# A piece of q moved from the plain load queue to the casting queue, and the beginning of an attention and SwiGLU kernel put in a new order

## Chip, cores, metric

One core of one Trainium2 chip. The metric is the device time of one execution in microseconds (us). Executions are compared by the mean of their fast runs; a run counts as slow when it is over 1.5% above the fastest of the same kernel. For every run the mean granted clock of TensorE is on record too (the share of its full clock that the engine was given, 1.00 being all of it), and it turns out to matter here. Times inside an execution are microseconds from the start of its span.

## The reference

```python
def _attn_ref(q, k, v):                    # each 8 x 8 x 576 x 64, float32
    def phi(x, c, s):                      # c, s: cosine and sine of pi/2 * position / 576
        r = np.maximum(x, 0.0)
        return np.concatenate([r * c, r * s], axis=-1)
    q_p, k_p = phi(q, cos_w, sin_w), phi(k, cos_w, sin_w)
    kv = np.einsum('bhsf,bhsd->bhfd', k_p, v)
    z = np.sum(k_p, axis=2)
    num = np.einsum('bhsf,bhfd->bhsd', q_p, kv)
    den = np.einsum('bhsf,bhf->bhs', q_p, z)[..., None] + 1e-06
    return num / den
# its output, as 4608 x 512, is the x of:
def _moe_ref(x, w_gate, w_val, w_out):     # 512 x 1536, 512 x 1536, 1536 x 512
    g = x @ w_gate
    return (g / (1 + np.exp(-g)) * (x @ w_val)) @ w_out
```

## The kernel before

The feed-forward products dominate, and TensorE is busy with them from about 18 us to the end. What concerns us is the beginning: until the first tiles of attention output (x) exist, TensorE has nothing to multiply. Loads come by two ways: SyncE's plain queue brings float32 (`first`), GpSimd's queue casts to bf16 on the way (`raw`). q of the first batch is cut into slots 0 to 8; two slots make one tile of 128 rows.

```python
    CUT = (4, 7)
    first = {"q": consts.tile([P, G, CUT[0], D], FP32, name="first_q")}
    # ... homes of the first v and k, float32, in buffers that are used later ...
    def load_first(nm, gs, lo=0, hi=NC):              # plain, no cast
        nc.sync.dma_start(out=first[nm][:, gs, lo:hi]..., in_=source(0, nm)[:, gs, lo * D:hi * D])
    load_first("v", slice(0, 2))
    load_first("v", slice(2, 4))
    load_first("q", slice(0, G), 0, 2)                # tile 0
    load_first("k", slice(0, 2))
    load_first("k", slice(2, 4), 0, KCUT)
    load_first("k", slice(2, 4), KCUT, NC)
    load_first("q", slice(0, G), 2, 4)                # tile 1, behind k
    # ...
    nc.gpsimd.tensor_copy(out=hold, in_=first["v"][:, 1, 0, 0:1])   # casting queue starts when v is there
    load_slots(0, "q", CUT[0], NW)                    # tiles 2 and 3, cast to bf16
    load_w(0, 1)                                      # then the weights
    # ...
    def turn_q(t):                                    # transposes of tile t
        ...
                if t < 2:                             # from the cast copy qf: 4 products of 128 columns
                    nc.tensor.transpose(out=ps[:, y]..., in_=qf[:, c, j]..., identity=ident)
                    continue
                for i in range(2):                    # from raw: 8 products with 64 columns as weights
                    nc.tensor.transpose(out=ps[i * D:(i + 1) * D, y], in_=raws[0, "q"][:, 2 * j + i, 2 * t + c], ...)
```

The order in which the engines get the work of the beginning is a list of words. `cq` casts a q slot, `tq` transposes a tile, `qr` relus it, `qw` weights it with cosine and sine, `rk` relus k, `kv` makes the k·v products, `kvo` copies them out, `a` makes a tile's attention products, `den`, `rec`, `x` divide, `xt` and `xc` transpose x and copy it, `G` and `V` are gate and value products, `s` and `m` silu and multiplication, and `z` are fillers: products with zeros that only keep TensorE busy.

```python
    words = """
        cq0@act cq1@act tq0 qr0@dve rk1.0@act rk0.0@dve qw0.0 qw0.1 z6 kv0.0 rk2.0@act rk3.0@dve rk2.1@act
        kv1.0 kvo01@dve rk3.1@act cq3@dve kv1.1 cq2@dve kvo00@dve tq1 kvo10@act a0.0 qr1@dve kvo11@act qw1.1
        z2 a0.1 qw1.0 tq2 den0 rec0 a1.0 x0.0 qr2@act tq3 x0.1 xt0.0 a1.1 qw2.0 xc0.0@act xt0.1 qw2.1
        xc0.1@act den1 z2 a2.0 rec1 qr3@act G1.0 ...
    """.split()
```

Gate and value products of narrow tiles share one accumulator bank:

```python
    def ffn_mm(tg, fc, lo=0, hi=GH, which=(0, 1)):
        # ...
                both = take(1, ("f", tg, fc, lo))
                st["f", tg, fc, lo] = [both[:, 0:n], both[:, n:2 * n]]    # gate half, value half
```

## Time and profile before

| | before |
|---|---|
| time, first three runs (median) | 327.97 us |
| span of the profiled run, its mean clock | 326.1 us, 1.00 |
| TensorE busy | 98% |
| k·v products end | 12.69 us |
| last piece of q (slots 2 and 3) lands, tile 1 starts | 13.67, 14.40 us |
| last product of the beginning ends | 30.17 us |
| first output product | 43.16 us |
| first long product group (512 columns) | 57.13 us |

The rows from the end of the k·v products on are the markers by which the runs below are compared. The page of a profile has mean shares; the beginning is read from the chain of work in order of time (who released whom), from the timeline (start, length, engine, line, and in brackets the idle time ahead and what ended it) and from the time that transfers took to land. In these views PE is TensorE and PEld its weight loads, DVE is VectorE, ACT ScalarE, POOL GpSimd, SP SyncE, a q behind the name the engine's instruction queue, and L316 line 316 of the kernel. The lines stand in the prediction.

### The profile page before, as it was taken

What the parts mean: (1) busy time and instruction counts of PE and PEld (TensorE: products, weight loads), DVE (VectorE), ACT (ScalarE), POOL (GpSimd) and SP (SyncE); (2) the same over time, 40 slices, a digit from 0 to 9 for tenths busy, and PEclk for the clock granted to TensorE, in tenths of its full rate; (3) what the DMA queues carried; (4) which work ended last, traced back from release to release, by engine and by line L of the source; (5) the groups of instructions that cost most, each with busy time, mean ns of one, the idle gap of its engine ahead of it and who ended that gap; (6) DMA issues with size and microseconds to landing.
All of it is one profiled execution on the core that took longest, in us unless ns stands there. A gap on an engine that the chain in (4) does not pass through costs nothing.

```text
span 326.1 us, 6192 instructions
## 1 busy us (share of the span) xinstructions
PE 318.7 (98%) x2459; PEld 165.0 (51%) x2470; DVE 182.3 (56%) x367; ACT 132.8 (41%) x248; POOL 34.1 (10%) x57
## 2 busy tenths in 40 slices
PE   8799999999999999999999999999999999999995
PEld 4488855454545444544454445444454445444443
DVE  7594857885575655575557555655664145423420
ACT  7353456843463336423543344343432133213311
POOL 6654300002001100020002000200000000000000
PEclk9999999999999999999999999999999999999999
DMA  7999999398867997799598949795921411140014
GB/s 259 224 199 197 207 204 211 62 132 137 162 117 95 163 140 146 110 157 158 121 124 127 181 110 136 108 184 116 138 51 34 99 32 32 36 105 21 2 32 97
DMA packets 71660, 40.51 MB, mean 124 GB/s; under 512 B 46672, under 2 KB 66384, under 8 KB 71632
## 3 DMA queue, kind: packets, MB, share of 16 engines
q1 hardware_dynamic: 49808, 22.55, 39.0%
q0 software_dynamic: 21664, 17.44, 35.2%
q8 instruction: 19, 0.31, 0.4%
q10 hardware_dynamic: 160, 0.13, 0.1%
q14 instruction: 9, 0.07, 0.1%
HBM read 37.75 MB, written 9.44 MB: 145 GB/s over the span
## 4 chain that ended last, share of the span: by engine, by line
PE 94%; DMA 3%; SPq 1%; issue 0%; ACT 0%; DVE 0%; ACTq 0%; DVEq 0%
PE banks L503 57%; PE banks L539 28%; DMA first_q<-in_q_dram 3%; PE banks L276 3%; PE banks L390 2%; SPq L116 1%; PE banks L475 1%; PE banks L434 1%; PE banks L372 1%; PE banks L558 1%; PE banks L264 0%; PE banks L149 0%; ACT ob L561 0%; PE banks L351 0%; DVE qf L339 0%
## 5 line engine op out<-in xcount | busy, mean ns | idle before, releaser
L514 DVE TENSOR_TENSOR ht<-sg,banks 128x512 bf16<-128x512 bf16 (+2 forms) x122 | 76.0, 625 | 67.2 <-PE banks L503 60.9
L509 ACT ACTIVATE sg<-banks 128x512 bf16<-128x512 f32 (+2 forms) x122 | 66.9, 548 | 113.8 <-PE banks L503 108.7
L503 PE MATMUL banks<-xT,wv_sb 128*128 128x512 bf16 (+2 forms) x488 | 112.8, 355 | 0.0
L503 PE MATMUL banks<-xT,wg_sb 128*128 128x512 bf16 (+2 forms) x488 | 112.8, 355 | 0.0
L539 PE MATMUL banks<-wo_sb,ht 128*128 128x512 bf16 x409 | 93.5, 379 | 0.6
L503 PEld LDWEIGHTS <-wv_sb 128*128 128x128 bf16 x488 | 47.1, 98 | 46.4
L503 PEld LDWEIGHTS <-wg_sb 128*128 128x128 bf16 x488 | 45.7, 98 | 41.5
L539 PEld LDWEIGHTS <-ht 128*128 128x128 bf16 x420 | 40.0, 98 | 45.2 <-issue 0.4
L546 ACT COPY ob<-banks 128x512 f32<-128x512 f32 x18 | 10.6, 586 | 51.4 <-PE banks L539 49.4
L232 DVE TENSOR_TENSOR r_q<-raw_q,tab 128x1152 bf16<-128x1152 bf16 x24 | 17.9, 753 | 20.2 <-ACT raw_q L215 20.2
L546 DVE COPY ob<-banks 128x512 f32<-128x512 f32 x17 | 11.7, 691 | 28.9 <-PE banks L539 28.0
L236 DVE TENSOR_TENSOR v<-raw_v,tab 128x1152 bf16<-128x1152 bf16 x31 | 23.0, 751 | 0.3 <-ACT raw_v L570 0.3
L411 DVE TENSOR_TENSOR x<-banks,rec 128x512 bf16<-128x512 f32 (+1 forms) x32 | 21.5, 674 | 1.1
L714 POOL COPY hold<-phit 1x2 bf16<-1x2 bf16 x5 | 0.9, 176 | 156.6 <-DMA phit<-r_q 156.6
L215 ACT ACTIVATE raw_k<-raw_k 128x576 bf16<-128x576 bf16 x24 | 16.0, 675 | 0.0
L215 ACT ACTIVATE raw_q<-raw_q 128x576 bf16<-128x576 bf16 x24 | 15.7, 680 | 0.5 <-DMA raw_q<-in_q_dram 0.5
L390 PEld LDWEIGHTS <-phit 128*128 128x128 bf16 (+1 forms) x240 | 9.9, 100 | 6.0 <-issue 1.3
L390 PE MATMUL banks<-kv,phit 128*128 128x65 bf16 (+1 forms) x240 | 11.5, 195 | 0.0
L149 PE MATMUL banks<-zeros 128*128 128x64 bf16 (+1 forms) x66 | 9.9, 310 | 1.0 <-DVE zeros L144 1.0
L299 DVE CAST kv<-banks 64x260 bf16<-64x260 f32 x12 | 5.1, 428 | 7.5 <-ACT kv L299 7.4
L276 PEld LDWEIGHTS <-raw_k 64*64 64x64 bf16 x504 | 7.5, 106 | 2.6 <-issue 2.1
L276 PE MATMUL banks<-v,raw_k 64*64 64x130 bf16 x504 | 8.7, 218 | 0.0
(80 smaller groups left out, 136.3 us busy)
## 6 DMA issues: line engine op xcount, KB each, us to landing
out_dram<-ob SPq DMA_DIRECT2D x70, 128.0 KB, 2.4
raw_k<-in_k_dram POOLq DMA_DIRECT2D x7, 576.0 KB, 9.7
raw_q<-in_q_dram POOLq DMA_DIRECT2D x6, 576.0 KB, 6.1
raw_v<-in_v_dram POOLq DMA_DIRECT2D x6, 576.0 KB, 12.3
wo_sb<-in_moe_w_out_dram POOLq DMA_DIRECT2D x3, 512.0 KB, 12.3
wg_sb<-in_moe_w_gate_dram POOLq DMA_DIRECT2D x5, 256.0 KB, 10.6
wv_sb<-in_moe_w_val_dram POOLq DMA_DIRECT2D x5, 256.0 KB, 10.0
wo_sb<-in_v_dram SPq DMA_DIRECT2D x2, 576.0 KB, 4.1
```

Source lines behind the costliest of these rows:

```text
L149: nc.tensor.matmul(out=ps, lhsT=zeros, rhs=zeros[:, 0:cols].unsqueeze(1).to_broadcast([P, 4, cols]), start=True, stop=True)
L215: nc.scalar.activation(out=out, in_=in_, func=AF.Relu)
L232: nc.vector.tensor_tensor(out=st[b, "q"][:, g], in0=o.unsqueeze(2).to_broadcast([P, NC, 2, D]), in1=tab, op=ALU.mult)
L236: nc.vector.tensor_tensor(out=v2s[b % 2][:, g, :, :, 0:D], in0=(first if b == 0 and g == 0 else {"v": raw_of(b, "v")})["v"][:, g].unsqueez ...
L276: nc.tensor.matmul(out=ps[i * D:(i + 1) * D, e, j * 2 * D1:(j + 1) * 2 * D1], lhsT=raws[b, "k"][es, g, c], rhs=v2s[b % 2][es, g, c, :, 0:D ...
L390: nc.tensor.matmul(out=ps[ms, e, g * D1:(g + 1) * D1], lhsT=phit[b][:, e, g, c:c + n].rearrange("p c s -> p (c s)"), rhs=kv2s[b % 2][:, e, ...
L411: nc.vector.tensor_tensor(out=st["x", t].rearrange("p (y e d) -> p e y d", e=2, d=D)[:, :, ys], in0=ps[:, :, 0:2 * J * D1].rearrange("p e ...
L503: nc.tensor.matmul(out=st["f", tg, fc, lo][i], lhsT=(wg_sb, wv_sb)[i][:, kc, fs], rhs=xT[tg][:, ts, kc], start=(kc == 0), stop=(kc == KC - 1))
L509: nc.scalar.activation(out=sg[:, 0:n], in_=st["f", tg, fc, lo][0], func=AF.Silu)
L514: nc.vector.tensor_tensor(out=hts[tg % 2][:, fc, r:r + n], in0=st.pop(("s", tg, fc, lo))[:, 0:n], in1=ps[1], op=ALU.mult)
L539: nc.tensor.matmul(out=o_ps[t], lhsT=hts[tg % 2][:, fc, r:r + P], rhs=wo_sb[:, fc], start=(fc == 0), stop=(fc == FC - 1))
L546: (nc.scalar.copy if t % 2 == 0 else nc.vector.tensor_copy)(out=ob, in_=ps)
```

## The change

Intent: load q's slots 2 and 3 by the casting queue, at its head, instead of uncast behind k; drop the two casts; and order the work of the beginning anew, from landings as measured. A third, smaller edit puts the two attention halves of the fourth tile back to back.

```diff
-    CUT = (4, 7)
+    QCUT = 2
+    CUT = 7
-    first = {"q": consts.tile([P, G, CUT[0], D], FP32, name="first_q")}
+    first = {"q": consts.tile([P, G, QCUT, D], FP32, name="first_q")}
-    load_first("q", slice(0, G), 2, 4)
-                if t < 2:
+                if t == 0:
-    load_slots(0, "q", CUT[0], NW)
+    load_slots(0, "q", QCUT, 4)
+    load_slots(0, "q", 4, NW)
     words = """
-        cq0@act cq1@act tq0 qr0@dve rk1.0@act rk0.0@dve qw0.0 qw0.1 z6 kv0.0 rk2.0@act rk3.0@dve rk2.1@act
-        kv1.0 kvo01@dve rk3.1@act cq3@dve kv1.1 cq2@dve kvo00@dve tq1 kvo10@act a0.0 qr1@dve kvo11@act qw1.1
-        z2 a0.1 ... V1.1 x3.0 s2.01 G0.1 V0.1 s0.1 V2.01 ...
+        cq0@act cq1@act tq0 qr0@dve qw0.0 qw0.1 rk1.0@act rk0.0@dve z8 kv0.0 rk3.0@dve rk2.0@dve kv1.0
+        kvo00@act rk3.1@dve kvo01@act rk2.1@dve kv1.1 tq1 kvo10@act kvo11@dve a0.0 qr1@dve a0.1 qw1.0 tq3
+        qw1.1 tq2 den0 ... G2.01 x3.0 G3.01 s2.01 m1.1 V2.01 ... G1.23 m0.23 G5.23 s1.23 V1.23 ...
         (the rest of both lists cut; renamings that follow from CUT cut too)
-    at((0, 0), lambda: kv_free(1), a_(4, 0))
-    at((0, 1), a_(4, 1))
+    at((0, 0), lambda: kv_free(1), a_(4, 0), a_(4, 1))
```

More of the change, by code (lines that the diff above doesn't have):

```diff
@@ L584 @@
     load(1, "v", 2)
-    load_slots(1, "q", 0, CUT[1])
+    load_slots(1, "q", 0, CUT)
     load_wo(0)
@@ L588 @@
     load_wo(2)
-    load_slots(1, "q", CUT[1], NC)
+    load_slots(1, "q", CUT, NC)
     for nm in ("q", "k", "v"):
@@ L610, in q_ @@
     def q_(b, j, part, eng="act"):
-        lo, hi = ((0, CUT[b]), (CUT[b], NC))[part]
+        lo, hi = ((0, CUT), (CUT, NC))[part]
         return lambda: qturn_pe(b, j, lo, hi, eng)
     words = """
-        cq0@act cq1@act tq0 qr0@dve rk1.0@act rk0.0@dve qw0.0 qw0.1 z6 kv0.0 rk2.0@act rk3.0@dve rk2.1@act
-        kv1.0 kvo01@dve rk3.1@act cq3@dve kv1.1 cq2@dve kvo00@dve tq1 kvo10@act a0.0 qr1@dve kvo11@act qw1.1
-        z2 a0.1 qw1.0 tq2 den0 rec0 a1.0 x0.0 qr2@act tq3 x0.1 xt0.0 a1.1 qw2.0 xc0.0@act xt0.1 qw2.1
-        xc0.1@act den1 z2 a2.0 rec1 qr3@act G1.0 x1.0 a2.1 G0.0 s1.0 V0.0 qw3.0 s0.0 xt1.0 qw3.1 V1.0
-        xc1.0@dve a3.0 a3.1 m0.0 G1.1 den3 G2.01 m1.0 s1.1 rec3 V1.1 x3.0 s2.01 G0.1 V0.1 s0.1 V2.01 m1.1
-        m0.1 xt3.0 den2 m2.01 G3.01 rec2 V3.01 x2.0 s3.01 G4.01 xc3.0@dve G5.01 s4.01 m3.01 xt2.0 s5.01
-        V4.01 xc2.0@dve V5.01 m4.01 G2.23 m5.01 G0.23 s2.23 V0.23 s0.23 G3.23 m0.23 V2.23 s3.23 G4.23 m2.23
-        V4.23 s4.23 V3.23 m4.23 G1.23 m3.23 V1.23 s1.23 G5.23 m1.23 V5.23 s5.23 m5.23
+        cq0@act cq1@act tq0 qr0@dve qw0.0 qw0.1 rk1.0@act rk0.0@dve z8 kv0.0 rk3.0@dve rk2.0@dve kv1.0
+        kvo00@act rk3.1@dve kvo01@act rk2.1@dve kv1.1 tq1 kvo10@act kvo11@dve a0.0 qr1@dve a0.1 qw1.0 tq3
+        qw1.1 tq2 den0 qr3@act rec0 x0.0 a1.0 a1.1 qr2@act x0.1 xt0.0 qw3.1 xt0.1 xc0.0@act qw3.0 xc0.1@act
+        den1 z2 a3.0 rec1 G1.0 x1.0 a3.1 s1.0 G0.0 V0.0 qw2.0 s0.0 xt1.0 qw2.1 V1.0 xc1.0@dve a2.0 a2.1 m1.0
+        G1.1 den3 den2 V1.1 rec3 s1.1 G2.01 x3.0 G3.01 s2.01 m1.1 V2.01 rec2 s3.01 x2.0 xt3.0 V3.01
+        xc3.0@act m2.01 xt2.0 m3.01 G5.01 xc2.0@dve G4.01 s5.01 m0.0 G0.23 s4.01 V0.23 s0.23 G1.23 m0.23
+        G5.23 s1.23 V1.23 s5.23 V4.01 m1.23 V5.23 m4.01 V5.01 m5.23 G2.23 m5.01 V2.23 s2.23 G3.23 m2.23
+        V3.23 s3.23 G4.23 m3.23 V4.23 s4.23 G0.1 m4.23 V0.1 s0.1 m0.1
     """.split()
```

## The prediction

> **What bounds the kernel now.** I read the page first, from the engine shares down to the chain that ended last. TensorE is busy almost everywhere, so only its own work, or time in which it has none, can change the end:
>
> ```profile
> PE 318.7 (98%) x2459; PEld 165.0 (51%) x2470; DVE 182.3 (56%) x367; ACT 132.8 (41%) x248; POOL 34.1 (10%) x57
> ...
> PE   8799999999999999999999999999999999999995
> ...
> PE 94%; DMA 3%; SPq 1%; issue 0%; ACT 0%; DVE 0%; ACTq 0%; DVEq 0%
> PE banks L503 57%; PE banks L539 28%; DMA first_q<-in_q_dram 3%; PE banks L276 3%; PE banks L390 2%; SPq L116 1%; PE banks L475 1%; PE banks L434 1%; PE banks L372 1%; PE banks L558 1%; PE banks L264 0%; PE banks L149 0%; ACT ob L561 0%; PE banks L351 0%; DVE qf L339 0%
> ```
>
> The only piece of the chain that is not TensorE work and not tiny is one transfer, first_q, 3% of 326.1 us. The chain listed in order of time shows where it lies (columns: start us, length us, what):
>
> ```profile
> 3.84 9.83 DMA first_q<-in_q_dram
> 13.67 0.03 issue
> ...
> 13.76 0.60 DVE qf L339 x2
> ...
> 14.40 0.40 PE banks L347 x4
> 14.80 0.33 PE banks L372 x4
> 15.13 0.43 PE banks L149 x2
> ```
>
> This is the last uncast piece of q, slots 2 and 3, issued by SyncE behind v, the first q piece and k. It lands at 13.67 us, VectorE casts it in two steps, and at 14.40 TensorE transposes it (second tile of q) and goes on to the attention products. From there to the end the chain is TensorE, piece after piece, so whatever moves 14.40 earlier moves the end, unless something later takes the time back. The timeline from 11.96 to 14.40 shows TensorE's idle time, and the row of L149 at 15.13 above is filler (products with zeros):
>
> ```profile
> 11.96 0.73 PE L316 MATMUL banks<-v,raw_k 64*64 64x130 bf16 x16 [0.31 <-ACT raw_k L215]
> 12.72 0.65 ACT L324 CAST kvd<-banks 128x260 bf16<-128x260 f32 x2 [0.51 <-PE banks L316]
> 13.76 0.58 DVE L339 CAST qf<-first_q 128x256 bf16<-128x256 f32 x2 [2.37 <-DMA first_q<-in_q_dram]
> 14.40 0.40 PE L347 MATMUL banks<-ident,qf 128*128 128x128 bf16 x4 [1.71 <-DVE qf L339]
> ```
>
> The k·v products end at 12.69, and TensorE then waits 1.71 us. That gap, and two fillers of 0.43 us at 15.13 and 17.52, is what there is to win before the feed-forward products fill the engine (unbroken from 18 us on). The transfers of the beginning, by their own view (KB, us from issue to landing):
>
> ```profile
> first_q<-in_q_dram SPq DMA_DIRECT2D x2, 256.0 KB, 7.8
> ...
> ht<-in_k_dram SPq DMA_DIRECT2D x1, 256.0 KB, 8.1
> raw_q<-in_q_dram POOLq DMA_DIRECT2D x1, 256.0 KB, 8.5
> ```
>
> The last k piece is issued at 3.33, its landing is at 11.47. The casting queue (GpSimd) starts with q's slots 4 to 7, issued at 4.50, landed at 13.04.
>
> [...] raw_q arrives as bf16 with no cast after it. [...] between 9 and 12 us both queues have packets in every microsecond (software queue 141, 200, 282; hardware queue 243, 203, 210). [...] Here the software queue's 528th packet (512 data packets and 16 for the semaphore) falls at about 11.65 and the landing at 13.04, so 1.4 us; I use 1.4.
>
> **The change part by part.**
>
> 1. *Landing of q slots 2 and 3.* The piece moves from the end of the hardware queue to the head of the software one. It has 512 data packets, like the piece that headed that queue before. At the packet rates above (6 before 9 us, then 141, 200, 282) the 528th comes at 11.65; its packets carry 256 B, and such packets took 40 ns against 59 ns for the 512 B ones, so perhaps 11.2. With 1.4 us: landing at 12.6 to 13.0, estimate 12.7. Before it was 13.67: 1.0 us earlier.
>
> 2. *The casts.* Two VectorE casts between landing and transpose go: 0.73 us (13.67 to 14.40) shrinks to about 0.1. Against that the second tile is now transposed in 8 products of 64 columns instead of 4 of 128; the third and fourth tile did it so and took 0.39 and 0.34 us start to start, against 0.34: at most 0.05 us lost.
>
> 3. *k.* Its last pieces are relued by VectorE one after the other instead of partly ScalarE. Last piece at 11.47, two relus of about 0.28, so k·v's last 16 products start at 12.1 and end at 12.5. So the piece at 12.7, not k, still starts the second tile, at 12.8: 1.6 us earlier than 14.40.
>
> 4. *q slots 4 to 7*, now second in the software queue, needed by the tile that follows at once. Bytes that must have been read by then: v and k 2.36 MB, q slots 0 to 7 1.05 MB, together 3.41 MB. In the kernel before, hardware packets to 12.0 us sum to 2.84 MB and software packets to 0.28 MB in bf16, 0.57 MB as read: 3.41. So it is read by 12.0 and lands at 13.4. Its transposes would follow at 12.8 + 0.4 + two attention halves at 0.23 = 13.7: no wait, 0.3 us to spare.
>
> 5. *Order.* I carried the new order through the three engines with the durations of the trace (0.22 us for four products of 128 columns, 0.44 for 256; relu of a tile 0.42 on VectorE, 0.60 on ScalarE; weighting 0.37; x 0.69; copy 0.43) and the old landings of the weights. Checked on the old order, this puts the end of the last beginning product at 30.52; the trace has 30.17. On the new order it gives 29.05 with the piece at 12.3 or sooner, 29.25 at 12.7, 29.75 at 13.2. So the gain is 30.52 - 29.25 = 1.27 us. Of the 1.6 us at the second tile, 0.3 is spent again on waits for VectorE chains of x, which no longer hide behind the late piece. One filler pair is moved ahead of k·v (8 products there instead of 6), where k's landing makes it free.
>
> 6. *Fourth tile's two halves back to back* at the first output slot: one switch less between 64-row and 128-row weight loads. The chain shows about 0.11 us more than the products themselves at each switch: 0.1 us gained.
>
> Sum: 1.27 + 0.1, some 1.4 us: 327.97 - 1.4 = 326.6.
>
> **Is it kept?** The weights' landings come from an unchanged total of bytes, so I keep them. In the carried order value weights for columns 2 and 3 (19.04) are used at 19.8 and gate weights for 4 and 5 (20.36) at 21.4: slack of 0.7 and 1.0 us where it was over 2. The output weights, landing at 40.82, 43.38 and 45.91, are used now at 43.16, 45.81 and 47.99; 1.4 us earlier still leaves 0.9, 1.0 and 0.7. The v of the second batch lands at 36.04 for a VectorE use at 39.3.
>
> **Rivals.**
>
> - *The wait changes its name.* The casting queue delivers no sooner: its first packet is seen near 8.8 although issued at 4.50, and 512 small packets could make the old 13.04. Then TensorE waits to 13.1, and the carried order ends near 29.7: gain 0.8 us, 327.1. For it: the fixed start. Against it: packets of half the size and a hardware queue that empties earlier.
> - *The second piece becomes the wait.* q's slots 4 to 7 land at 14.5 instead of 13.4; the carried order ends at 29.74: again some 0.8 us. The byte count speaks against it.
> - *Weights become the wait.* With slack of 0.7 us, a software queue behind by one more transfer of 1 us would hold V for columns 2 and 3: at worst all of the gain is lost, 328.0. Against it: the queue has up to eight transfers outstanding all the time, and a transfer less stands in the other queue.
> - *More than I think.* Should the piece land by 12.3, and no chain of x wait: the gap and fillers give up to 2.1 us, 325.9.
>
> **Range and chances.** 326.6 in the middle; 325.9 from the last rival; 327.7 from the first three with a run-to-run spread of 0.6 us (327.35 to 328.61). 2% would be 6.6 us, and the whole idle and filler time of TensorE behind the first transpose is under 5 us, so neither side is in reach: within 2% has 0.97, faster 0.02, slower 0.01.
>
> **What would show it.** Step 1: landing of the raw_q piece of 128 KB at 12.6 to 13.0, and no first_q in the chain behind 8 us. Step 2: 14.40 becomes about 12.8, with no VectorE qf row. Step 4: the transposes of raw_q for the third and fourth tile at 13.7 without a wait on a DMA. Step 5: last product of the beginning at about 28.8 (30.17 less 1.37), feed-forward groups everywhere earlier by that much, and no wait on wv_sb or wg_sb. Wrong would be: a wait on raw_q over 0.5 us, PE idle between 14 and 20 us over 1 us, or a shift at 30 us that is gone at 60 us.

## The result, and the profile after

The first measurement gave 326.05 us (median of 4 runs, 325.69 to 326.35) against 328.29 us (4 runs, 327.35 to 328.61). The ratio was 0.9936, with a 95% interval of 0.9911 to 0.9961. A ratio here is the mean of one kernel's fast runs over the mean of the other's fast runs of the same rounds, so it isn't quite the ratio of the medians. Repeated on other occasions, the changed kernel's 16 fast runs average 325.96 us.

| marker | before | after | difference |
|---|---|---|---|
| q slots 2 and 3 land | 13.67 | 11.71 | -1.96 |
| k·v products end | 12.69 | 12.70 | 0 |
| tile 1 starts | 14.40 | 12.63 | -1.77 |
| last product of the beginning ends | 30.17 | 28.75 | -1.42 |
| first output product | 43.16 | 41.74 | -1.42 |
| first long product group | 57.13 | 55.48 | -1.65 |
| span | 326.1 | 324.6 | -1.5 |

The transfers that the casting queue got first, in the transfer view of the changed kernel for 4.4 to 6.1 us (issued at 5.40 and 4.51; KB, us to landing):

```profile
raw_q<-in_q_dram POOLq DMA_DIRECT2D x1, 256.0 KB, 7.6
raw_q<-in_q_dram POOLq DMA_DIRECT2D x1, 128.0 KB, 7.2
```

The piece is there at 11.71, and slots 4 to 7 at 13.05, where they were before. TensorE's timeline of the changed kernel at the place of the old gap:

```profile
11.98 0.72 PE L316 MATMUL banks<-v,raw_k 64*64 64x130 bf16 x36
12.63 0.41 PE L351 MATMUL banks<-ident,raw_q 128*64 128x128 bf16 x8
12.98 0.64 PE L372 MATMUL banks<-kvd,qwT 128*128 128x130 bf16 x8
13.54 0.64 PE L351 MATMUL banks<-ident,raw_q 128*64 128x128 bf16 x16
```

The 1.71 us are gone: the transposes follow the k·v products at once, and no row has a wait in brackets. The chain of work shows what took the transfer's place:

```profile
12.05 0.71 PE banks L316 x32
...
12.78 0.43 DVE kvd L324
13.21 0.34 DVE qr L217
...
13.58 0.76 DVE qwT L360 x2
14.34 0.09 DVE den L399
...
14.45 0.21 DVE rec L406
...
14.69 0.44 DVE x L411
...
15.17 0.29 PE banks L475 x2
```

From the end of k·v to the first transpose of x (L475) the chain is now VectorE's, step after step. Before 12 us it runs through k·v, the fillers and back to q's first piece; no q transfer ends it later than 8 us.

One thing the two profiles can't tell: the means differ by more than 1.65 us, and the times of the kernel before come in two clusters. That became a question of its own below.

### The profile page after: what moved, and what is told of

Read it like the earlier page. It is cut to its first block, busy times and chain, and to the rows that moved or that the text cites. A ratio compares the mean times of both kernels' runs of the same rounds, so it can differ in the third digit from the quotient of the medians.

```text
span 324.6 us, 6212 instructions
## 1 busy us (share of the span) xinstructions
PE 318.0 (98%) x2474; PEld 164.6 (51%) x2474; DVE 181.8 (56%) x366; ACT 132.3 (41%) x247; POOL 34.8 (11%) x58
## 4 chain that ended last, share of the span: by engine, by line
PE 95%; DMA 2%; DVE 1%; ACT 0%; SPq 0%; issue 0%; ACTq 0%
PE banks L503 58%; PE banks L539 28%; PE banks L276 3%; PE banks L390 2%; DMA first_q<-in_q_dram 2%; PE banks L475 1%; PE banks L434 1%; PE banks L149 1%; PE banks L558 1%; PE banks L264 0%; PE banks L316 0%; PE banks L372 0%; SPq L117 0%; DVE qwT L360 0%; ACT ob L561 0%; ACT qf L339 0%
## 5 line engine op out<-in xcount | busy, mean ns | idle before, releaser
L149 PE MATMUL banks<-zeros 128*128 128x64 bf16 (+1 forms) x66 | 8.7, 290 | 1.0 <-DVE zeros L144 1.0
## 6 DMA issues: line engine op xcount, KB each, us to landing
wo_sb<-in_moe_w_out_dram POOLq DMA_DIRECT2D x3, 512.0 KB, 12.7
```

What stands on the lines that cost most here:

```text
L149: nc.tensor.matmul(out=ps, lhsT=zeros, rhs=zeros[:, 0:cols].unsqueeze(1).to_broadcast([P, 4, cols]), start=True, stop=True)
```

## The experiments

Twelve runs. Single profiles of kernels with the same loads have transfers landing up to 1.4 us apart (the last k piece at 10.07 to 11.84 us over all traces), which shifts the whole beginning. The trace records every landing in 16 parts, and the last part counts: in the kernel before, the parts of slots 2 and 3 landed from 11.62 to 13.67 us, and their cast started at 13.76. For the piece of q at the head of the casting queue the first part came at 10.06 to 10.20 us in eight traces of the new loads, the last at 10.57 to 11.97. So I compare distances between markers inside one trace, and mean times over runs.

### The changed kernel again

No edit. 

> The changed kernel again, so that the parts below are timed on the same chip. Every theory: 0.992 to 0.996 of the kernel before (its first measurement was 0.9936); piece of q slots 2 and 3 lands at 11.5 to 12.0 us, last product of the beginning ends near 28.8, first long product group near 55.7.

325.99 us mean of 6 runs against 328.09 (35 runs of the kernel before): ratio 0.9933. The piece landed at 11.63, tile 1 started at 12.51, first long group at 55.37. It repeats.

### The queue move alone

```diff
 (the changed kernel, with)
-    words of the changed kernel
+    words of the kernel before, without cq3@dve and cq2@dve
-    at((0, 0), lambda: kv_free(1), a_(4, 0), a_(4, 1))
+    at((0, 0), lambda: kv_free(1), a_(4, 0))
+    at((0, 1), a_(4, 1))
```

> The queue move alone: q slots 2 and 3 by the casting queue, with the old order of the beginning (only the two casts taken out) and the two halves of the fourth tile apart as before. Theory A (the piece's wait was the cost, the new order adds little): the last product of the beginning, 30.17 us in the kernel before and 28.75 in the changed one, ends at 28.4 to 28.8, and the time is that of the changed kernel but for the 0.2 us of the fourth tile: ratio to before 0.995. Carried through the three engines with the landings of the changed kernel's trace, the old order even ends 0.7 us sooner than the new one. Theory B (the new order is what turns the earlier landing into time): ends at 29.6 or later, ratio 0.998 or above.

325.84 us mean (6 runs), ratio 0.993: all of the gain, without the new order. Theory B falls. The profiled run was one of early landings (k at 10.31, the piece at 10.89), so its absolute markers say little; the distance from the last k·v product to the first output product was 28.70 us, against 29.04 in the changed kernel: half of the 0.7 us that I expected of the old order.

### The new order alone

```diff
 (the kernel before, with the words of the changed kernel and)
-    kv1.1 tq1
+    kv1.1 cq3@dve cq2@dve tq1
```

> The new order alone, with q slots 2 and 3 uncast behind k as before and their two casts put just ahead of the second tile's transposes. Theory A: the piece still lands near 13.7, the second tile starts near 14.4, and the last product of the beginning ends at 30.1 to 30.7 (carried: 0.3 us later than the old order): ratio 0.999 to 1.001. Theory B: it ends at 29.5 or sooner, ratio 0.998 or below.

328.40 us mean (14 runs), ratio 1.0009 (0.9994 to 1.0024). The piece landed at 13.79 and tile 1 started at 14.44, as before. Alone, the order gains nothing. But this profile was an odd one: the last k·v product ended at 12.64, tile 1 started 1.8 us later, and then the first output product came at 44.28, not 43.16. The windows view (busy us and instructions by engine; the number behind POOL's is the granted clock, then the transfers' share and GB/s) shows why:

```profile
13.00:14.00 1.00, 0.00 (x0) 0.00 (x0) 0.12 (x1) 0.06 (x1) 0.74 (x1) 1.00 1.80 181
14.00:15.00 1.00, 0.56 (x10) 0.57 (x11) 0.84 (x4) 0.00 (x0) 0.62 (x1) 1.00 1.78 182
15.00:16.00 1.00, 1.00 (x23) 0.70 (x20) 0.97 (x3) 0.00 (x0) 0.99 (x3) 0.89 1.50 199
16.00:17.00 1.00, 0.95 (x9) 0.76 (x9) 0.93 (x5) 0.81 (x2) 0.60 (x1) 0.50 1.47 194
17.00:18.00 1.00, 1.00 (x7) 0.40 (x6) 1.00 (x4) 0.92 (x3) 0.60 (x1) 0.50 1.45 195
18.00:19.00 1.00, 1.00 (x9) 0.81 (x8) 0.93 (x4) 0.06 (x1) 0.88 (x2) 0.50 1.45 196
19.00:20.00 1.00, 1.00 (x19) 1.00 (x17) 0.66 (x2) 0.28 (x1) 0.57 (x1) 0.90 1.44 196
```

TensorE did nothing from 13 to 14 us, and two microseconds later its clock went to half for some 3.4 us (15.78 to 19.19 in the clock records): 9, 7 and 9 matmuls in a microsecond, where the kernel before has 20, 13 and 21. The first output product came 31.64 us after the last k·v product, against 30.47 in the kernel before, and the last product of the beginning ended at 31.29, outside the expected 30.1 to 30.7. I took this for a second cost of the same gap, one that my prediction did not have.

### The fourth tile alone

```diff
-    at((0, 0), lambda: kv_free(1), a_(4, 0))
-    at((0, 1), a_(4, 1))
+    at((0, 0), lambda: kv_free(1), a_(4, 0), a_(4, 1))
 (in the kernel before)
```

> The kernel before with only the two halves of the fourth tile put back to back. The distance from the last product of the beginning (30.17) to the first long product group (57.29) is 27.12 in the kernel before and 26.90 in the changed one. Theory A (that 0.22 us is the one switch of weight form saved): distance 26.9, time 0.2 us less, ratio 0.999. Theory B (the 0.22 is from elsewhere): distance 27.1, ratio 1.000. The times alone can hardly tell 0.2 us; the distance in the trace is what counts.

Between the first output product and the first long group there are 13.97 us in the kernel before and 13.75 in this one (13.74 in the changed kernel, 13.97 with the queue move alone): theory A, 0.22 us. The time, 327.53 us mean of 21 fast runs and a ratio of 0.9984 (0.9972 to 0.9995), agrees within its spread; one of 22 runs, at 419.58 us and a clock of 0.752, was in a slow state and is not counted.

### The clock, read over all runs

Every run's mean clock is recorded. The 82 timed runs of the kernel before fall into two groups, with nothing between 0.995 and 0.997:

| kernel before, fast runs | number | mean time |
|---|---|---|
| mean clock 0.997 to 1.000 | 44 | 327.62 us |
| mean clock 0.992 to 0.995 | 38 | 328.89 us |
| all | 82 | 328.21 us |

One stretch of 3.41 us at half clock, as in the trace above, is 1.7 of 326 us, a mean clock of 0.995 from this stretch alone (that run has 0.993 on record); the lower group, 0.992 to 0.995, is what such a trace gives. Of 16 runs of the changed kernel none is in the lower group. That is still only a correlation: filling the gap without shortening the wait tests it.

### Gap filled, wait left

```diff
 (the kernel before)
-    ... kv1.1 cq2@dve kvo00@dve tq1 ...
+    ... kv1.1 z7 cq2@dve kvo00@dve tq1 ...
```

> The kernel before with seven more products with zeros in the 1.7 us gap between k-v and the second tile, and nothing else. They cannot make the work path shorter: the second tile still waits for the piece of q (13.7 us). Theory C (besides the wait itself, the idle gap lets the granted clock fall to half for some 3 us in part of the executions: 13 of the 35 timed runs of the kernel before have a mean clock of 0.992 to 0.995 and take 328.83 us on average, the other 22 take 327.65; of 16 runs without the gap none has it): no run of this kernel under 0.997, mean near 327.6, ratio 0.9985. Theory D (the low clock comes from elsewhere, by chance): a third of the runs stays low, ratio 1.000.

The timeline of TensorE in this run:

```profile
11.87 1.68 PE L149 MATMUL banks<-zeros 128*128 128x512 bf16 x7
13.48 0.40 PE L347 MATMUL banks<-ident,qf 128*128 128x128 bf16 x4
```

The fillers lie where the gap was, and tile 1 still follows the late piece (12.84 in this run, tile 1 at 13.48). 327.47 us mean of 21 runs, none with a clock under 0.998, against 328.18 with 15 of 32 in the lower group in the same rounds: ratio 0.9977 (0.9965 to 0.9989). Theory C holds, theory D falls. Seven products with zeros, no work at all, gain 0.7 us on the mean.

### Queue move and fourth tile, old order

```diff
 (the queue move alone, and)
-    at((0, 0), lambda: kv_free(1), a_(4, 0))
-    at((0, 1), a_(4, 1))
+    at((0, 0), lambda: kv_free(1), a_(4, 0), a_(4, 1))
```

> The queue move and the fourth tile's halves together, with the old order of the beginning. If the three parts add up as in the first four runs (queue move: all of the gain; order: none or slightly against; fourth tile: 0.2 us), it takes 0.2 to 0.5 us less than the changed kernel: from the last k-v product to the first output product 22.8 us and not 23.1, ratio to before 0.992. If the new order is worth something that the luck of early landings hid in the queue-only profile, it is slower than the changed kernel: ratio 0.995.

325.65 us mean (6 runs), ratio 0.992; 28.70 us from the last k·v product to the first output product. With a second set of six runs (below) the mean of 12 is 325.71 us against 325.96 for the changed kernel's 16. Its chain of work, where the k·v products start the stretch:

```profile
3.34 7.80 DMA ht<-in_k_dram
11.14 0.02 issue
11.16 0.73 ACT raw_k L215 x2
11.89 0.04 issue
11.94 0.42 PE banks L316 x14
12.36 0.34 PE banks L351 x8
```

Here the landing of the last k piece and ScalarE's two relus of it lead, and tile 1 follows k·v directly. (The 22.8 and 23.1 us of the expectation are not this distance; only their difference of 0.3 can be compared.) The 0.34 us between the two orders can be found in the traces. In the changed kernel TensorE's timeline has

```profile
18.73 1.04 PE L503 MATMUL banks<-xT,wg_sb 128*128 128x256 bf16 x8
19.80 0.60 PE L503 MATMUL banks<-xT,wv_sb 128*128 128x256 bf16 x4
...
22.87 1.04 PE L503 MATMUL banks<-xT,wg_sb 128*128 128x256 bf16 x8
23.94 0.49 PE L503 MATMUL banks<-xT,wv_sb 128*128 128x256 bf16 x3
```

Eight gate products of 256 columns take 0.87 us start to start, so 18.73 should be followed at 19.60 and 22.87 at 23.74; each time 0.20 us are lost. Both times it is a value product whose silu is issued just ahead of it in the new list (`s2.01 m1.1 V2.01`, `s1.23 V1.23`). In the trace's records these value products wait for the semaphore that ScalarE's silus raise, and the silus ahead of them end at 19.75 and 23.89 us, just before 19.80 and 23.94. Gate and value share a bank. In the old list the silu stands further ahead. Summed from start to start between the two markers, the gate and value products take 21.58 us in the changed kernel and 21.28 here. Transposes and attention products take 0.35 us more in the changed kernel, waits for VectorE included, and its fillers 0.32 less, since one pair was moved ahead of k·v: these two cancel. I did not run a list with only these words moved, so the shares are read from the trace, not tested.

### The casting queue's first two transfers swapped

```diff
-    load_slots(0, "q", QCUT, 4)
-    load_slots(0, "q", 4, NW)
+    load_slots(0, "q", 4, NW)
+    load_slots(0, "q", QCUT, 4)
```

> The changed kernel with the casting queue's first two transfers swapped: q slots 4 to 7 first, then slots 2 and 3. Theory E (the landing of the piece, at the head of the queue, is what freed the second tile): slots 4 to 7 land near 12.4 and slots 2 and 3 near 13.0; the second tile starts at 13.1 and not 12.6, and the products of the beginning end 0.2 to 0.5 us later than in the changed kernel; ratio 0.995. It also tells what set the piece's early landing (11.7, my estimate was 12.7): in the changed kernel the casting queue moved 400 packets of 256 B between 9 and 10 us, in the kernel before 141 of 512 B. If the small packets do it, the head transfer here goes at 140 to 250 packets per us and lands after 12.2; if the shorter plain queue does it, at about 400 and lands before 12.0.

326.34 us mean (6 runs), 0.4 us over the changed kernel; the piece landed at 12.14 and tile 1 started at 12.19, behind k·v by 0.25 us. Theory E holds in direction and size, though this profile was one of early landings again. For the packets, I set the head transfer's landing against the last k piece's of the same trace: 1.2 to 2.2 us behind it where 512 B packets head the casting queue and the plain queue still has q (four traces of kernels with the old loads), 1.0 us with 512 B packets and the shorter plain queue (this run), 0.3 to 0.6 us with 256 B packets and the shorter plain queue (eight traces). So both reasons seem to count. By the test that I had set, this run was undecided: the head transfer landed at 11.41, before 12.0 as for the shorter plain queue, but at 269 packets between 9 and 10 us, close to what I expected of the small packets. The first of its 16 parts landed at 10.68, against 11.62 to 11.83 with the old loads and 10.06 to 10.20 with 256 B packets at the head, which gives the shorter plain queue the larger share. One trace for the middle case is thin.

### No fillers ahead of k·v

```diff
-    ... rk0.0@dve z8 kv0.0 ...
+    ... rk0.0@dve kv0.0 ...
```

> The changed kernel without the eight products with zeros ahead of k-v, which its chain of work counts with 1.7 us. Theory C: they cost nothing (k-v starts when the relu of k ends, 10.96 us in the changed kernel, fillers end at 10.7), but without them TensorE stands idle for 1.4 us or more, and part of the runs has a clock under 0.997 and takes 1 us longer; k-v still starts at 11.0. Theory F (the fillers are on the path): k-v starts sooner, at 10.3 to 10.8, and the runs of full clock are 0.2 to 0.6 us faster than the changed kernel's 326.0.

The first k·v product in TensorE's timeline of this run:

```profile
10.88 0.72 PE L316 MATMUL banks<-v,raw_k 64*64 64x130 bf16 x36 [1.70 <-DVE raw_k L217]
```

It starts at 10.88, as in the changed kernel (10.88 to 11.00), so the fillers are not on the path, although the chain counts them with 1.73 us: they and the relu of k end together. But 1.70 us of idleness brought 4 of 10 runs into the lower clock group (326.90 us; the six others 325.98). Theory C again, from the other side: a gap put in makes the slow runs, as a gap filled takes them out.

### How long a gap it takes

```diff
 (the changed kernel)                     (the kernel before)
-    ... rk0.0@dve z8 kv0.0 ...           -    ... kv1.1 cq2@dve ...
+    ... rk0.0@dve z4 kv0.0 ...           +    ... kv1.1 z3 cq2@dve ...
```

> The changed kernel with four fillers ahead of k-v in place of eight: TensorE's idle gap there becomes some 0.8 us (0 to 0.2 with eight, 1.7 with none, where 4 of 10 runs had a clock under 0.997). If any gap sends the clock down with a chance that grows with its length, 1 or 2 of 10 runs are low; if there is a least length over 0.8 us, none is. Runs of full clock: 326.0 us, as with eight and with none, for the fillers are not on the path.

> The kernel before with three fillers in its 1.7 us gap in place of none (28 of 67 runs low) or seven (0 of 21 low): some 1.0 us of idleness is left. Chance growing with length: about a fifth of the runs low; a least length over 1.0 us: none low. Runs of full clock: 327.5 to 327.6.

With four fillers the gap ahead of k·v was 0.88 us: none of 6 runs low, 325.72 us. With three fillers in the old gap an estimated 1.0 us was left (1.71 less three at 0.22): none of 9 fast runs low, 327.43 us (its profiled run was in a slow state, clock 0.85 from end to end, 373.87 us, and is not used). Gaps of 1.7 us had 38 of 82, 8 of 14, 5 of 21 and 4 of 10 low. With a chance of a fifth, 15 runs without a low one would come up some 4 times in 100 (0.8 to the 15th), so a chance that is simply proportional to the gap is unlikely but not excluded, and whether there is a limit, and where between 1.0 and 1.7 us, is open. The changed kernel has a gap of its own, ahead of tile 0, of 1.31 us in its first profile, 0.64 in the last and none in the second; none of its 16 runs was low.

### Both candidates once more

No edits. 

> The queue move and the fourth tile's halves with the old order, again, beside the changed kernel on the same chip. The traces have 28.70 us from the last k-v product to the first output product against 29.04 with the new order, so 0.3 us less: 325.65 against 326.0, no run low. If the first difference was chance, both are at 326.0.

> The changed kernel a third time, as the other side of the run before this one: 326.0 us, no run with a clock under 0.997.

325.78 us with the old order and 325.87 with the new (6 runs each). Over all runs the difference is 0.24 us in favour of the old order, with a standard error of 0.14 (from the spreads of 0.43 and 0.24 over 12 and 16 runs): not clear of chance in the times. The distance in the traces has the same sign and did not change much (28.70 and 28.71 us in the two old-order traces, 29.04 in all three of the new). The best version I ran is thus the queue move with the fourth tile's edit and the old order, by a margin that only the traces resolve. Part of it is lost again further on: in its two traces the output product at 45.73 and 46.19 us starts 0.06 and 0.18 us late, just after the third load of the output weights has landed, so that from the last k·v product to the first long group they take 42.50 and 42.62 us, against 42.78 or 42.79 in the changed kernel (where these weights are 0.5 us early). Those weights are the next thing in the way. In these last rounds the ratios to the kernel before were 0.991, mainly because 10 of its 15 runs were of the lower clock.

## Why the prediction was right, and where its steps were off

The forecast 326.6 us (325.9 to 327.7) held: 326.05. By its own steps:

1. *Landing of the piece: 12.7 us.* It was 11.71. The direction was right and the size off by 1.0 us: I took the casting queue's packet rate from a trace in which larger packets headed that queue and the plain queue still had the same q piece to carry. At 9 to 10 us the casting queue moved 141 packets of 512 B (59 ns each) in the kernel before and 400, mostly of 256 B (41 ns each), in the changed one, beside 243 and 155 of the plain queue. The start was the same: first packets at 8.89 and 8.96 us, some 4.4 us after the issues at 4.50 and 4.51. The queue's 528th packet came at 10.26, not at 11.2 to 11.65. The 1.4 us that I added from that packet to the landing came out again (10.26 to 11.71 is 1.45), but I had misread it: packets of the next transfer were among the 528. By their sizes, the last packet of the head transfer starts at 12.66 in the kernel before, 0.4 us ahead of the landing at 13.04, and at 11.25 in the changed one, 0.5 us ahead of 11.71. The rival "the wait changes its name" (13.1) did not come.
2. *The casts.* Gone as said. The eight transposes that replace four take 0.35 us to the next product (12.63 to 12.98), as estimated.
3. *k.* I had k·v end at 12.5 and the piece start tile 1 at 12.8. k·v ended at 12.70 and set the start (12.63), with all 36 products of the second half, 0.72 us, behind the last relu, and not 16; the piece was early enough to cost nothing. So the wait that I had as the last one (the piece) and the one that was (k·v) changed places, and that the two errors nearly cancel (12.8 against 12.63) is luck: by the trace a landing anywhere from 11.71 to 12.6 is hidden behind k·v.
4. *Slots 4 to 7: 13.4 without a wait.* 13.05, transposed at 13.54 without a wait.
5. *The order carried through: a gain of 1.27 us, the beginning over at about 28.8, 0.3 us spent again.* It ended at 28.75, 1.42 us sooner, and the start of tile 1 came 1.77 us sooner, of which 0.35 was spent again by the first output product. The size was right; the reason only in part: the waits for chains of x on VectorE are there, but the filler pair moved away pays for them, and what is left, as the traces read, is chiefly the two waits of value products behind silus.
6. *Fourth tile: 0.1.* 0.22 us, shown by the run of that part alone.

The sum in the trace is 1.77 - 0.35 + 0.22 = 1.64, against my 1.4. No weight became a wait in the changed kernel.

**What no step had** is the clock. The change is worth 328.21 - 325.96 = 2.25 us on the mean. Of this, 327.62 - 325.96 = 1.66 is the work moved sooner, as in the trace; the other 0.59 is that 38 of 82 runs of the kernel before have a mean clock of 0.992 to 0.995 and take 1.27 us longer (0.46 x 1.27 = 0.59), and the changed kernel has no gap as long. My profile of before happened to be one of full clock, and I called the spread of 327.35 to 328.61 a run-to-run spread; by the later runs it was two kinds of run (the clocks of those first four are not on record). I also counted the "new order" as part of the gain; the run with the queue move alone shows that it isn't.

What decides which runs are hit, the traces do not show. In the trace of the new order alone TensorE was busy for 1.62 of the 3.42 us before the dip (12.36 to 15.78); in the profile of before, with nearly the same gap, it was busy for 1.76 of the 3.41 us from 12.76 to 16.17, and no dip followed. Why the clock drops stays open; that the gap brings the low clock about is shown: with the gap filled 0 of 21 runs were low, against 15 of 32 without, and a gap of 1.70 us put in ahead of k·v made 4 of 10 low, against 0 of 16 in the changed kernel.

## What to carry to other kernels

Where one engine bounds a kernel from some point on, find the one wait that decides when that point is reached, and ask next what stands right behind it: here the piece could by the trace have come 0.9 us later at no cost, because k was next. Read the mean clock of every run before you call a spread noise: here, with an idle gap of 1.7 us on TensorE, 38 of 82 runs took 1.27 us more at a mean clock of 0.992 to 0.995, and with seven products with zeros in the gap none of 21 was low. When several edits come together, run each alone: one of three carried nearly all, one a little, and one, by the traces, went slightly the wrong way.
